# The tail of a decode block: gate's matmuls on two columns scaled afterwards, the last two heads straight into wo's rows, and the last diagonal in halves

## The chip, the cores and the metric

The kernel runs on one core of a Trainium2 chip. The metric is device time in microseconds (us); each timed run is one execution of the whole kernel, and the median of several is compared.

## The reference

One token goes through a conditioned transformer block: D = 640, 32 heads of 128, a cache of 16384 positions for each head, and a feed-forward layer of F = 1728.

```python
mod = silu(c) @ w_mod                         # six vectors: sa, ca, ga, sb, cb, gb
h = layernorm(x) * (1 + ca) + sa
q = h @ wq                                    # 32 heads x 128
o[head] = softmax(q[head] @ K[head].T / sqrt(128)) @ V[head]
x = x + ga * (concat(o) @ wo)
h = layernorm(x) * (1 + cb) + sb
x = x + gb * ((silu(h @ w_gate) * (h @ w_up)) @ w_down)
```

The caches are 268 of the 290 MB that are read.

## The kernel before

Every operation is recorded with the operations that it depends on, and each engine then runs its own in the order in which the program recorded them. An engine waits for a semaphore of another engine, or of a transfer, before an instruction that needs it. The order on each engine is therefore the order of the source, and an instruction whose input is late holds back all that stand behind it on that engine.

Heads go in 16 pairs. For a pair, K (8.4 MB) is loaded into one of two buffers (`load_k`), DVE multiplies it by q and folds it (`score`), PE finishes the sum (`reduce_mm`), and the largest score and the exponentials follow (`largest`, `weigh`). V (8.4 MB) has a single buffer, so its load waits until PE has read the V before it (`load_v`). `pv` multiplies the weights by V into `acc_ps`, ACT copies that to `acc_sb` (L473), and `diag` picks each head's own part with small float32 matmuls into `OT_ps` (L482). Pairs 1 to 14 run in a loop on PE; pair 15 (`PL`, `NP - 1`) is written out, with its V loaded in four pieces.

All large loads are issued by SP in the order of the source. In the last stretch that is: V of pair 14, `dma_wo0` (24 heads' rows) and `dma_wo3` (8 heads' rows) after the scores of pair 14, the four pieces of the last V once PE has finished with V of pair 14, and after the scores of pair 15 gate's weights (`dma_wg`), up's in two pieces (`dma_wu0`, `dma_wu1`) and down's in four (`dma_wd0` to `dma_wd3`).

The product with wo needs the heads' outputs laid out as wo's rows were loaded. `GROUPS` says how: a group (h0, n) holds n heads, and each partition holds n consecutive rows of wo, 1280 bytes each. The outputs are divided by their sums (`on`), spread by a mask into `Z` on DVE (`z_op`, L617), turned by a matmul each (`lay`, L630), copied to `A_sb` by ACT (L633), and then multiplied by wo (`project`, L645: five matmuls of one column for each head, all into `attn_ps`). The first four groups are done while the last V is on its way. Group 4, heads 28 to 31, waits for the last pair: on_last, z, am, as, and 20 matmuls.

Then ACT copies the attention output (`attn_bf`, L688), DVE scales it by `ga` and adds x, and `layernorm_ops` (L360 to L377) makes the second normalisation: PE sums over partitions (`ln2_tot`, L362), DVE centres (`ln2_xc`, L364), ACT squares (L367), PE sums again (`ln2_tot2`, L369), ACT takes Ln and Exp for the reciprocal deviation (L371, L374). DVE scales and shifts (L694, L697) to `h2_col`, clears the sums of gate and up (L698, L699), and PE multiplies by gate (70 matmuls of one column), up (56 and 14; all at L709) and, after the silu on ACT and DVE, by down (L730, four groups of 20, 20, 20 and 10, each of which waits for its own piece of the weights).

Of the kernel before, what the change touches and what calls it, by code (L numbers as in the profile page):

```python
# [6 lines left out]
BF16 = mybir.dt.bfloat16  # L7
# [200 lines left out]
def build(nc, A_x, A_k, A_v, A_wq, A_wo, B_wg, B_wu, B_wd, c_in, w_mod, out):  # L208
    H, S, Dh = A_k.shape[1], A_k.shape[2], A_k.shape[3]
    D = A_x.shape[2]  # L210
# [10 lines left out]
    assert FT % 2 == 0 and FT // 2 <= 128  # L221
    FR = FT // 2
    FCH = 4 * NB + 2
    GROUPS = [(0, 8), (8, 8), (16, 8), (24, 4), (28, 4)]
    QW = 32
    QR = 16

# [1 line left out]
    with es:  # L229
# [5 lines left out]
        def sb(name, shape, dtype):  # L235
            return es.enter_context(nc.sbuf_tensor(name, list(shape), dtype))
# [20 lines left out]
        negid = sb("negid", [128, 64], F32)  # L257
        d2 = sb("d2", [128, 64], F32)
        sel = sb("sel", [128, 8], F32)
        msk = {n: sb("msk%d" % n, [128, 128 // n], F32) for n in (8, 4)}  # L260
        e8 = {n: sb("e%d" % n, [128, n], BF16) for n in (8, 4)}
        Z = sb("Z", [128, H // 8 + 1, 128], BF16)
        A_sb = sb("A_sb", [128, H], BF16)
        rows = sb("rows", [1, 2, D], BF16)
        pm = sb("pm", [128, NP], F32)
        nb = sb("nb", [128, NP], F32)
        rsz = sb("rsz", [128, H], F32)
# [20 lines left out]
        tt2 = sb("tt2", [128, KC], F32)  # L288
        tt3 = sb("tt3", [128, KC], F32)
        h2_col = sb("h2_col", [128, KC], BF16)  # L290
        eg = sb("eg", [128, FCH], F32)
        dg = sb("dg", [128, FCH], F32)
        rg = sb("rg", [128, FCH], F32)
# [63 lines left out]
        o_rr = op(DVE, lambda e: e.reciprocal(out=rr[:], in_=dd[:]), deps=[o_dd], name="rr")  # L357
        o_sc = op(DVE, lambda e: e.tensor_tensor(out=silu_c[:], in0=c_col[:], in1=rr[:], op=ALU.mult), deps=[o_rr, o_cc], name="silu_c")

        def layernorm_ops(src_f32, src_dep, sum_ap, c0, tag, xc_t, free=None):  # L360
            st_ps = misc
            o_tot = op(PE, lambda e: e.matmul(st_ps[:, c0:c0 + 1], lhsT=ones_f[:], rhs=sum_ap, start=True, stop=True),  # L362
                       deps=[src_dep, o_onesf, free], name=tag + "_tot")
            o_xc = op(DVE, lambda e: e.scalar_tensor_tensor(  # L364
                out=xc_t[:], in0=src_f32[:], scalar=float(D), in1=st_ps[:, c0:c0 + 1].broadcast_to([128, KC]),
                op0=ALU.mult, op1=ALU.subtract), deps=[o_tot, src_dep], name=tag + "_xc")
            o_sq = op(ACT, lambda e: e.activation(  # L367
                out=junk[:], in_=xc_t[:], func=ACTF.Square, accum_out=st[:, c0 + 1:c0 + 2]), deps=[o_xc], name=tag + "_sq")
            o_tot2 = op(PE, lambda e: e.matmul(st_ps[:, c0 + 1:c0 + 2], lhsT=ones_f[:], rhs=st[:, c0 + 1:c0 + 2], start=True, stop=True),  # L369
                        deps=[o_sq], name=tag + "_tot2")  # L370
            o_ln = op(ACT, lambda e: e.activation(  # L371
                out=st[:, c0 + 2:c0 + 3], in_=st_ps[:, c0 + 1:c0 + 2], func=ACTF.Ln, scale=1.0 / float(D) ** 3, bias=EPS),
                deps=[o_tot2], name=tag + "_ln")
# [37 lines left out]
        o_h = op(DVE, lambda e: e.tensor_tensor(out=h_col[:], in0=tt1[:], in1=mod_ps[:, 0:KC], op=ALU.add), deps=[o_t1], name="h_col")  # L411
        o_modc = op(ACT, lambda e: e.activation(out=modb[:], in_=mod_ps[:, 2 * KC:6 * KC], func=ACTF.Copy), deps=[o_mod, o_h], name="mod_b")
        o_onep_b = op(DVE, lambda e: e.tensor_scalar_add(out=onep_b[:], in0=modb[:, 2 * KC:3 * KC], scalar1=1.0), deps=[o_modc], name="onep_b")
        ga, sb_, gb = modb[:, 0:KC], modb[:, KC:2 * KC], modb[:, 3 * KC:4 * KC]


# [42 lines left out]
        def pv(p):  # L459
            cuts = VCUT if p == NP - 1 else [0, T2]  # L460
            prev = None
            for c, (a, b) in enumerate(zip(cuts, cuts[1:])):
                def f_pv(e, p=p, a=a, b=b):
                    last = None
                    for j in range(a // 4, b // 4):
                        s = j % 4
                        last = e.matmul(acc_ps[32 * s:32 * s + 8, :], lhsT=PZ[:, p % 2, j, :],  # L467
                                        rhs=vbuf[:, 4 * j:4 * j + 4, :].rearrange("p t d -> p (t d)"),
                                        start=(j < 4), stop=(j >= NCH - 4), tile_position=(0, 32 * s))
                    return last  # L470
                prev = op(PE, f_pv, deps=[o_exp[p], d_v[p][c], o_acc[p - 1] if p >= 1 else o_accz, prev], name="pv%d_%d" % (p, c))
            o_pv[p] = prev
            o_acc[p] = op(ACT, lambda e: e.activation(out=acc_sb[:], in_=acc_ps[:], func=ACTF.Copy),  # L473
                          deps=[o_pv[p], o_diag[p - 1] if p >= 1 else None], name="acc%d" % p)

# [2 lines left out]
        def diag(p):  # L478
            def f_diag(e):
                last = None  # L480
                for i in range(4):
                    last = e.matmul(OT_ps[:, 0:2], lhsT=acc_sb[:, 128 * i:128 * (i + 1)], rhs=sel[:, i:8:4],  # L482
                                    start=(i == 0), stop=(i == 3))
                return last
            o_diag[p] = op(PE, f_diag, deps=[o_acc[p], o_sel, o_ot[p - 1] if p >= 1 else o_xf], name="diag%d" % p)
            if p < NP - 1:
                o_ot[p] = op(ACT, lambda e: e.activation(  # L487
                    out=OT_sb[:, 2 * p:2 * p + 2], in_=OT_ps[:, 0:2], func=ACTF.Copy), deps=[o_diag[p]], name="ot%d" % p)

        def reduce_mm(p, c, fold):  # L490
            def f_R(e):
# [87 lines left out]
        while a < len(GROUPS):  # L579
# [7 lines left out]
            for i in range(a, b):  # L587
                d_wo[i] = d
            a = b

# [57 lines left out]
            return op(PE, f_wo, deps=[o_as[g], d_wo[g]] + o_qev[-1], name="wo%d" % g)  # L648

        NG = len(GROUPS)  # L650
        lay(list(range(NG - 1)))
# [20 lines left out]

        for g in range(NG - 1):
            project(g)
        pv(NP - 1)
        diag(NP - 1)
        o_onl = op(DVE, lambda e: e.tensor_tensor(out=on_f[:, LAST:H], in0=OT_ps[:, 0:2], in1=rl[:, LAST:H], op=ALU.mult),  # L679
                   deps=[o_rl, o_diag[NP - 1]], name="on_last")  # L680
        for g, o in z_op(LAST, H, o_onl, "b"):
            o_z.setdefault(g, []).append(o)
        lay([NG - 1])
        o_wo = project(NG - 1)

        o_abf = op(ACT, lambda e: e.activation(out=attn_bf[:], in_=attn_ps[:, 0:KC], func=ACTF.Copy), deps=[o_wo], name="attn_bf")  # L688
# [4 lines left out]
        o_xc1, o_rstd1 = layernorm_ops(x1, o_x1, st[:, 4:5], 4, "ln2", xc1, o_rl)  # L693
# [4 lines left out]
        o_zg = op(DVE, lambda e: e.memset(g_ps[:, 0:FCH], 0.0), deps=[o_exp[NP - 2]], name="zero_g")  # L698
        o_zu = op(DVE, lambda e: e.memset(u_ps[:, 0:FCH], 0.0), deps=[o_exp[NP - 1]], name="zero_u")  # L699

        def chunk(j):
            return (slice(512 * (j // 4) + j % 4, 512 * (j // 4) + 512, 4), 128) if j < 4 * NB else (slice(512 * NB + j % 4, F, 2), FR)

        def f_gu(e, wv, ps_t, k0, k1):
            last = None
            for k in range(k0, k1):
                for j in range(FCH):
                    cols, w = chunk(j)
                    last = e.matmul(ps_t[0:w, j:j + 1], lhsT=wv[:, k, cols], rhs=h2_col[:, k:k + 1],  # L709
                                    start=(k == 0 and j == 0), stop=(k == KC - 1 and j == FCH - 1), skip_group_check=True)  # L710
            return last
        o_g = op(PE, lambda e: f_gu(e, wg_v, g_ps, 0, KC), deps=[o_h2, d_wg, o_zg], name="gate")
        o_u0 = op(PE, lambda e: f_gu(e, wu_v, u_ps, 0, UK), deps=[o_h2, d_wu[0], o_zu], name="up0")
        o_u = op(PE, lambda e: f_gu(e, wu_v, u_ps, UK, KC), deps=[o_h2, d_wu[1], o_u0], name="up1")
        o_eg = op(ACT, lambda e: e.activation(out=eg[:], in_=g_ps[:, 0:FCH], func=ACTF.Exp, scale=-1.0), deps=[o_g], name="eg")
        o_dg = op(DVE, lambda e: e.tensor_scalar_add(out=dg[:], in0=eg[:], scalar1=1.0), deps=[o_eg], name="dg")
        o_rg = op(DVE, lambda e: e.reciprocal(out=rg[:], in_=dg[:]), deps=[o_dg], name="rg")
        o_sg = op(DVE, lambda e: e.tensor_tensor(out=sg[:], in0=g_ps[:, 0:FCH], in1=rg[:], op=ALU.mult), deps=[o_rg, o_g], name="sg")
# [67 lines left out]
```

## Time and profile before

| | |
|---|---|
| median of 3 runs | 686.59 us (686.27 to 686.76) |
| the profiled execution, its own time | 686.55 us |
| its span in the profile | 684.6 us |
| outside the span | 1.95 us |
| granted TensorE clock, mean | 0.60 |
| DVE busy | 509.8 us, 74% |
| PE busy | 366.3 us, 54% |
| read from HBM | 290.47 MB, 424 GB/s over the span |
| packets of SP's queue | 98.4% of 16 engines' time |

The span is the time from the first to the last instruction of the profiled execution; its own time has what lies around it as well. All positions below are microseconds from the span's start. In the stretches after 640 us the granted clock is 0.50. The chain of waits is followed back from the last instruction, and each step of it is what released the one after it.

### The profile page before, as it was taken

To read this page: it belongs to the slowest core of one execution; us is meant where nothing else is said; L and a number is where in the kernel's file an instruction comes from. 1 tells how busy PE (TensorE), PEld (TensorE's weight loads), DVE (VectorE), ACT (ScalarE), POOL (GpSimd) and SP (SyncE) were. 2 spreads that over 40 slices of the span, in tenths; PEclk is the share of its full clock that TensorE was granted. 3 is DMA by queue.
4 is the path that set the end of the run, shared out by engine and by line. 5 is a ranking of instruction groups with operands and counts; after the bars stand their busy time and mean duration, and the time that the engine had idled before them with its cause. 6 is when DMAs were issued, how large, how long until landed. Compare 5 with 4: busy or idle time off the path is not lost.

```text
span 684.6 us, 5113 instructions
## 1 busy us (share of the span) xinstructions
PE 366.3 (54%) x2282; PEld 152.5 (22%) x2283; DVE 509.8 (74%) x179; ACT 45.8 (7%) x145; POOL 0.7 (0%) x6
## 2 busy tenths in 40 slices
PE   2522265646648173756637183745638184654765
PEld 2311122222212021221212121221212122222525
DVE  2079998959595977959595987959596986999200
ACT  1120000000000000100000000100000000100100
POOL 0000000000000000000000000000000000000000
PEclk9975565655556565565656565655656565655655
DMA  9999999999999999999999999999999999999994
GB/s 381 427 458 426 429 429 429 434 433 429 460 437 433 429 429 433 433 429 429 429 437 433 429 452 444 433 429 429 433 429 433 429 429 433 425 440 414 430 421 169
DMA packets 7422, 290.62 MB, mean 425 GB/s; under 512 B 914, under 2 KB 916, under 8 KB 1908
## 3 DMA queue, kind: packets, MB, share of 16 engines
q1 hardware_dynamic: 7408, 290.48, 98.4%
q8 instruction: 7, 0.11, 0.1%
q14 instruction: 3, 0.02, 0.0%
q10 hardware_dynamic: 4, 0.00, 0.0%
HBM read 290.47 MB, written 0.00 MB: 424 GB/s over the span
## 4 chain that ended last, share of the span: by engine, by line
DMA 52%; DVE 35%; PE 12%; issue 0%; ACT 0%; SPq 0%; DVEq 0%
DMA kring<-in_A_k_cache_dram 44%; DVE kring L503 16%; DVE kring L507 8%; DMA vbuf<-in_A_v_cache_dram 8%; PE psb L494 7%; DVE kring L512 4%; DVE kring L518 3%; DVE kring L524 2%; PE psb L467 2%; PE psb L709 1%; PE psb L532 1%; PE psb L730 0%; DVE pm L538 0%; PE psb L482 0%; SPq L80 0%
## 5 line engine op out<-in xcount | busy, mean ns | idle before, releaser
L503 DVE TENSOR_TENSOR kring<-kring,qbc 128x16384 bf16<-128x16384 bf16 x28 | 243.3, 8689 | 95.0 <-DMA kring<-in_A_k_cache_dram 95.0
L494 PE MATMUL psb<-kring,ident 128*128 128x256 bf16 x448 | 197.4, 607 | 124.1 <-DVE kring L512 124.1
L507 DVE TENSOR_TENSOR kring<-kring 128x8192 bf16<-128x8192 bf16 x28 | 123.8, 4420 | 0.5
L494 PEld LDWEIGHTS psb<-kring,ident 128*128 128x128 bf16 x448 | 51.7, 121 | 254.0 <-DVE kring L512 133.7
L467 PE MATMUL psb<-vbuf,PZ 128*8 128x512 bf16 x1024 | 84.6, 500 | 11.7 <-DMA vbuf<-in_A_v_cache_dram 11.5
L542 PE MATMUL psb<-d,bd_f 128*128 128x64 f32 x32 | 11.0, 447 | 113.8 <-ACT d L540 113.8
L512 DVE TENSOR_TENSOR kring<-kring 128x4096 bf16<-128x4096 bf16 x28 | 64.0, 2287 | 0.5
L518 DVE TENSOR_TENSOR kring<-kring,qbc 128x16384 bf16<-128x16384 bf16 x4 | 34.7, 8687 | 16.2 <-DMA kring<-in_A_k_cache_dram 16.2
L467 PEld LDWEIGHTS psb<-vbuf,PZ 128*8 128x8 bf16 x1024 | 27.3, 105 | 73.2 <-issue 53.4
L542 PEld LDWEIGHTS psb<-d,bd_f 128*128 128x128 f32 x32 | 8.0, 311 | 115.5 <-DVE pm L538 58.1
L532 PE MATMUL psb<-kring,ident 128*128 128x128 bf16 x64 | 14.5, 393 | 35.9 <-DVE kring L524 35.9
L524 DVE TENSOR_TENSOR kring<-kring 128x8192 bf16<-128x8192 bf16 (+2 forms) x12 | 31.7, 2646 | 0.3
L482 PEld LDWEIGHTS psb<-sel,acc_sb 128*128 128x128 f32 x128 | 29.3, 319 | 8.4 <-issue 4.3
L482 PE MATMUL psb<-sel,acc_sb 128*128 128x2 f32 x128 | 26.4, 328 | 1.4 <-ACT acc_sb L473 1.4
L473 ACT ACTIVATE acc_sb<-psb 128x512 f32<-128x512 f32 x16 | 9.6, 597 | 222.2 <-PE psb L467 222.2
L550 ACT ACTIVATE PZ<-psb,nb 64x256 bf16<-64x256 f32 x32 | 15.0, 469 | 63.0 <-DVE nb L546 62.8
L532 PEld LDWEIGHTS psb<-kring,ident 128*128 128x128 bf16 x64 | 7.4, 121 | 42.3 <-DVE kring L524 37.0
L679 DVE TENSOR_TENSOR on_f<-psb,rl 128x2 f32<-128x2 f32 x1 | 0.2, 159 | 20.6 <-PE psb L482 20.6
L540 ACT ACTIVATE d<-negid,pm 128x64 f32<-128x64 f32 x16 | 5.6, 348 | 139.1 <-DVE pm L538 139.1
L426 PE MATMUL psb<-vbuf,h_col 128*128 128x512 bf16 x39 | 10.1, 425 | 7.8 <-DMA vbuf<-in_A_wq_dram 7.8
L487 ACT ACTIVATE OT_sb<-psb 128x2 f32<-128x2 f32 x15 | 2.6, 172 | 158.5 <-PE psb L482 158.5
L403 PE MATMUL psb<-silu_c,kring 128*128 128x1 bf16 x150 | 6.2, 178 | 4.5 <-DMA kring<-in_w_mod_dram 4.5
(82 smaller groups left out, 86.2 us busy)
## 6 DMA issues: line engine op xcount, KB each, us to landing
kring<-in_A_k_cache_dram SPq DMA_DIRECT2D x4, 4096.0 KB, 37.6
vbuf<-in_A_wq_dram SPq DMA_DIRECT2D x1, 5120.0 KB, 27.1
kring<-in_w_mod_dram SPq DMA_DIRECT2D x1, 4800.0 KB, 14.1
vbuf<-in_A_v_cache_dram SPq DMA_DIRECT2D x1, 4096.0 KB, 16.4
kring<-in_A_wo_dram SPq DMA_DIRECT2D x1, 3840.0 KB, 29.2
kring<-in_B_w_gate_dram SPq DMA_DIRECT2D x1, 2160.0 KB, 25.9
vbuf<-in_A_v_cache_dram SPq DMA_DIRECT2D x1, 2048.0 KB, 20.9
kring<-in_B_w_down_dram SPq DMA_DIRECT2D x3, 640.0 KB, 32.6
```

What stands on the lines that cost most here:

```text
L426: last = e.matmul(q_ps[b][:, 0:512], lhsT=h_col[:, k:k + 1].broadcast_to([128, 128]), rhs=wq_v[:, k, g * 512:(g + 1) * 512], start=(k == 0 ...
L467: last = e.matmul(acc_ps[32 * s:32 * s + 8, :], lhsT=PZ[:, p % 2, j, :], rhs=vbuf[:, 4 * j:4 * j + 4, :].rearrange("p t d -> p (t d)"), st ...
L482: last = e.matmul(OT_ps[:, 0:2], lhsT=acc_sb[:, 128 * i:128 * (i + 1)], rhs=sel[:, i:8:4], start=(i == 0), stop=(i == 3))
L494: last = e.matmul(S_ps[p % 2][:, 0:T2], lhsT=ident[:], rhs=kring[:, p % 2, :, d], start=(d == 0), stop=(d == QW + QR - 1))
L503: o_m = op(DVE, lambda e: e.tensor_tensor(out=kv4, in0=kv4, in1=q4, op=ALU.mult), deps=[d_k[p][-1]] + o_qev[p // 2], name="mult%d_%d" % (p ...
L507: o_f = op(DVE, lambda e: e.tensor_tensor(out=kv4[:, :, 0], in0=kv4[:, :, 0], in1=kv4[:, :, 1], op=ALU.add), deps=[o_m], name="fold%d_%d" ...
L512: return op(DVE, lambda e: e.tensor_tensor(out=lo[:, :, 0:QR], in0=lo[:, :, 0:QR], in1=lo[:, :, QR:QW], op=ALU.add), deps=[o_f], name="fol ...
L518: o = op(DVE, lambda e: e.tensor_tensor(out=kv, in0=kv, in1=qbc[:, p, :].unsqueeze(1).broadcast_to([128, KCUT[c + 1] - KCUT[c], 128]), op= ...
L524: o = op(DVE, lambda e, w=w: e.tensor_tensor(out=kv[:, :, 0:w], in0=kv[:, :, 0:w], in1=kv[:, :, w:2 * w], op=ALU.add), deps=[o], name="fol ...
L532: last = e.matmul(S_ps[p % 2][:, KCUT[c]:KCUT[c + 1]], lhsT=ident[:], rhs=kring[:, p % 2, KCUT[c]:KCUT[c + 1], d], start=(d == 0), stop=(d ...
L542: o_mx[p] = op(PE, lambda e: e.matmul(mx_ps[:, 0:64], lhsT=bd_f[:], rhs=d2[:], start=True, stop=True), deps=[o_d2, o_bd1, o_bd2, o_nb[p - ...
L550: o_exp[p] = op(ACT, lambda e, half=half, ps=ps: e.activation(out=PZ[ps, p % 2, :, 4 * half:4 * half + 4], in_=S_ps[p % 2][ps, 0:T2].rearr ...
```

## The change

Five things change, and all but the first are in the last stretch.

- At the start, the two input rows are kept in the space of `qbc`, a third mask and selector (for n = 2) are made on DVE, and the shift of the second normalisation is copied to the second column of a new tile `ab` (640 x 2 values as 128 x 5 x 2).
- The last group of `GROUPS` shrinks to heads 28 and 29, so wo's last 1280 KB come in three transfers: 640 KB (group 3, 5120 bytes a partition), 320 KB (group 4, 2560 bytes a partition) and the last two heads as 320 KB, one row of 1280 bytes for each partition and head (`dma_wol`). All 30 heads are laid out and multiplied before the last V's products.
- The last pair's copy of `acc_ps` and its diagonal are done in two halves. on_last writes the divided outputs straight into `A_sb`, and ten matmuls (`wo_last`) finish the product.
- attn_bf is made by DVE instead of ACT, and the two clearing memsets stand before it.
- Gate is no longer multiplied by the finished `h2_col`, but by two columns side by side: the centred input times (1 + cb), and the shift. The first 14 of its matmuls (`gate0`) stand on PE between ln2's two totals, the other 56 after the second. Two operations on DVE then scale the first result by the reciprocal deviation and add the second. Up still uses `h2_col`.

```diff
-    GROUPS = [(0, 8), (8, 8), (16, 8), (24, 4), (28, 4)]
+    GROUPS = [(0, 8), (8, 8), (16, 8), (24, 4), (28, 2)]
...
+        o_abs = op(DVE, lambda e: e.tensor_copy(out=ab[:, :, 1], in_=modb[:, KC:2 * KC]), deps=[o_modc], name="ab_shift")
...
             o_sq = op(ACT, lambda e: e.activation(
                 out=junk[:], in_=xc_t[:], func=ACTF.Square, accum_out=st[:, c0 + 1:c0 + 2]), deps=[o_xc], name=tag + "_sq")
+            if between:
+                between(o_xc)
             o_tot2 = op(PE, ...)
...
+        def diag_last():
+            p, last = NP - 1, o_diag[NP - 2]
+            copies = [op(ACT, lambda e, h=h: e.activation(
+                out=acc_sb[:, 256 * h:256 * h + 256], in_=acc_ps[:, 256 * h:256 * h + 256], func=ACTF.Copy),
+                deps=[o_pv[p], last], name="acc%d_%d" % (p, h)) for h in range(2)]
+            for h in range(2):
+                def f_diag(e, h=h):
+                    out = None
+                    for i in (2 * h, 2 * h + 1):
+                        out = e.matmul(OT_ps[:, 0:2], lhsT=acc_sb[:, 128 * i:128 * (i + 1)], rhs=sel[:, i:8:4],
+                                       start=(i == 0), stop=(i == 3))
+                    return out
+                o_diag[p] = op(PE, f_diag, deps=[copies[h], o_sel, o_ot[p - 1]], name="diag%d_%d" % (p, h))
+            return o_diag[p]
...
+        d_wol = dma(wo_v[:, H - 2:H, :], A_wo[(H - 2) * 128:H * 128, :].rearrange("(h p) n -> p h n", p=128), "wol", deps=[o_R[NP - 2]], name="dma_wol")
...
-        pv(NP - 1)
-        diag(NP - 1)
-        o_onl = op(DVE, lambda e: e.tensor_tensor(out=on_f[:, LAST:H], in0=OT_ps[:, 0:2], in1=rl[:, LAST:H], op=ALU.mult),
-                   deps=[o_rl, o_diag[NP - 1]], name="on_last")
-        for g, o in z_op(LAST, H, o_onl, "b"):
-            o_z.setdefault(g, []).append(o)
-        lay([NG - 1])
-        o_wo = project(NG - 1)
+        pv(PL)
+        o_onl = op(DVE, lambda e: e.tensor_tensor(out=A_sb[:, LAST:H], in0=OT_ps[:, 0:2], in1=rl[:, LAST:H], op=ALU.mult),
+                   deps=[o_rl, diag_last()], name="on_last")
+        def f_wol(e):
+            last = None
+            for k in range(LAST, H):
+                for cc in range(KC):
+                    last = e.matmul(attn_ps[:, cc:cc + 1], lhsT=wo_v[:, k, cc:D:KC], rhs=A_sb[:, k:k + 1],
+                                    start=False, stop=(k == H - 1 and cc == KC - 1), skip_group_check=True)
+            return last
+        o_wo = op(PE, f_wol, deps=[o_onl, d_wol], name="wo_last")
...
-        o_abf = op(ACT, lambda e: e.activation(out=attn_bf[:], in_=attn_ps[:, 0:KC], func=ACTF.Copy), deps=[o_wo], name="attn_bf")
+        o_zg = op(DVE, lambda e: e.memset(g_ps[:, 0:2 * FCH], 0.0), deps=[o_exp[NP - 2]], name="zero_g")
+        o_zu = op(DVE, lambda e: e.memset(u_ps[:, 0:FCH], 0.0), deps=[o_exp[NP - 1]], name="zero_u")
+        o_abf = op(DVE, lambda e: e.tensor_copy(out=attn_bf[:], in_=attn_ps[:, 0:KC]), deps=[o_wo], name="attn_bf")
...
+        def gate0(o_xc1):
+            o_a = op(DVE, lambda e: e.tensor_tensor(out=ab[:, :, 0], in0=xc1[:], in1=onep_b[:], op=ALU.mult),
+                     deps=[o_xc1, o_onep_b, o_abs], name="ab_a")
+            o_g0.append(op(PE, lambda e: f_gu(e, wg_v, g_ps, ab_f, 2, 0, 1), deps=[o_a, d_wg, o_zg], name="gate0"))
+        o_xc1, o_rstd1 = layernorm_ops(x1, o_x1, st[:, 4:5], 4, "ln2", xc1, o_rl, gate0)
...
-        o_g = op(PE, lambda e: f_gu(e, wg_v, g_ps, 0, KC), deps=[o_h2, d_wg, o_zg], name="gate")
+        o_g = op(PE, lambda e: f_gu(e, wg_v, g_ps, ab_f, 2, 1, KC), deps=o_g0, name="gate")
...
+        gp = g_ps[:, 0:2 * FCH].rearrange("p (j n) -> p j n", n=2)
+        o_gt = op(DVE, lambda e: e.tensor_scalar_mul(out=sg[:], in0=gp[:, :, 0], scalar1=st[:, 7:8]), deps=[o_g, o_rstd1], name="gate_r")
+        o_gs = op(DVE, lambda e: e.tensor_tensor(out=g_sb[:], in0=gp[:, :, 1], in1=sg[:], op=ALU.add), deps=[o_gt], name="gate_s")
+        o_eg = op(ACT, lambda e: e.activation(out=eg[:], in_=g_sb[:], func=ACTF.Exp, scale=-1.0), deps=[o_gs], name="eg")
```

More of the change, by code (lines that the diff above doesn't have):

```diff
@@ L259, in build @@
         sel = sb("sel", [128, 8], F32)
-        msk = {n: sb("msk%d" % n, [128, 128 // n], F32) for n in (8, 4)}
-        e8 = {n: sb("e%d" % n, [128, n], BF16) for n in (8, 4)}
+        msk = {n: sb("msk%d" % n, [128, 128 // n], F32) for n in (8, 4, 2)}
+        e8 = {n: sb("e%d" % n, [128, n], BF16) for n in (8, 4, 2)}
         Z = sb("Z", [128, H // 8 + 1, 128], BF16)
         A_sb = sb("A_sb", [128, H], BF16)
-        rows = sb("rows", [1, 2, D], BF16)
+        rows = qbc[0:1].rearrange("p a d -> p (a d)")[:, 0:2 * D].rearrange("p (j n) -> p j n", j=2)
         pm = sb("pm", [128, NP], F32)
@@ L290, in build @@
         h2_col = sb("h2_col", [128, KC], BF16)
+        ab = sb("ab", [128, KC, 2], BF16)
+        g_sb = sb("g_sb", [128, FCH], F32)
         eg = sb("eg", [128, FCH], F32)
@@ L358, in build, with layernorm_ops @@
         o_sc = op(DVE, lambda e: e.tensor_tensor(out=silu_c[:], in0=c_col[:], in1=rr[:], op=ALU.mult), deps=[o_rr, o_cc], name="silu_c")
-        def layernorm_ops(src_f32, src_dep, sum_ap, c0, tag, xc_t, free=None):
+        def layernorm_ops(src_f32, src_dep, sum_ap, c0, tag, xc_t, free=None, between=None):
             st_ps = misc
@@ L472, in pv @@
             o_pv[p] = prev
+            if p == NP - 1:
+                return
             o_acc[p] = op(ACT, lambda e: e.activation(out=acc_sb[:], in_=acc_ps[:], func=ACTF.Copy),
@@ L485, in diag @@
             o_diag[p] = op(PE, f_diag, deps=[o_acc[p], o_sel, o_ot[p - 1] if p >= 1 else o_xf], name="diag%d" % p)
-            if p < NP - 1:
-                o_ot[p] = op(ACT, lambda e: e.activation(
-                    out=OT_sb[:, 2 * p:2 * p + 2], in_=OT_ps[:, 0:2], func=ACTF.Copy), deps=[o_diag[p]], name="ot%d" % p)
+            o_ot[p] = op(ACT, lambda e: e.activation(
+                out=OT_sb[:, 2 * p:2 * p + 2], in_=OT_ps[:, 0:2], func=ACTF.Copy), deps=[o_diag[p]], name="ot%d" % p)
+        def diag_last():
[12 more added lines that the diff above has]
+            return o_diag[p]
         def reduce_mm(p, c, fold):
@@ L650, in build @@
         NG = len(GROUPS)
-        lay(list(range(NG - 1)))
+        lay(list(range(NG)))
         largest(PL)
@@ L671, in build @@
                         B_wd[512 * NB:F, :].rearrange("(p r) n -> p (r n)", r=2), ("wd", NB), deps=wdeps, name="dma_wd%d" % NB))
-        for g in range(NG - 1):
+        for g in range(NG):
             project(g)
-        pv(NP - 1)
-        diag(NP - 1)
-        o_onl = op(DVE, lambda e: e.tensor_tensor(out=on_f[:, LAST:H], in0=OT_ps[:, 0:2], in1=rl[:, LAST:H], op=ALU.mult),
-                   deps=[o_rl, o_diag[NP - 1]], name="on_last")
-        for g, o in z_op(LAST, H, o_onl, "b"):
-            o_z.setdefault(g, []).append(o)
-        lay([NG - 1])
-        o_wo = project(NG - 1)
-        o_abf = op(ACT, lambda e: e.activation(out=attn_bf[:], in_=attn_ps[:, 0:KC], func=ACTF.Copy), deps=[o_wo], name="attn_bf")
+        pv(PL)
[12 more added lines that the diff above has]
+        o_abf = op(DVE, lambda e: e.tensor_copy(out=attn_bf[:], in_=attn_ps[:, 0:KC]), deps=[o_wo], name="attn_bf")
         o_ga = op(DVE, lambda e: e.tensor_tensor(out=tt2[:], in0=attn_bf[:], in1=ga, op=ALU.mult), deps=[o_abf, o_modc], name="ga_attn")
@@ L692, in build, with chunk, f_gu @@
             deps=[o_ga, o_xf], name="x1")
-        o_xc1, o_rstd1 = layernorm_ops(x1, o_x1, st[:, 4:5], 4, "ln2", xc1, o_rl)
+        def chunk(j):
+            return (slice(512 * (j // 4) + j % 4, 512 * (j // 4) + 512, 4), 128) if j < 4 * NB else (slice(512 * NB + j % 4, F, 2), FR)
+        def f_gu(e, wv, ps_t, src, n, k0, k1):
+            last = None
+            for k in range(k0, k1):
+                for j in range(FCH):
+                    cols, w = chunk(j)
+                    last = e.matmul(ps_t[0:w, n * j:n * j + n], lhsT=wv[:, k, cols], rhs=src[:, n * k:n * k + n],
+                                    start=(k == 0 and j == 0), stop=(k == KC - 1 and j == FCH - 1), skip_group_check=True)
+            return last
+        ab_f = ab[:].rearrange("p k n -> p (k n)")
+        o_g0 = []
+        def gate0(o_xc1):
[3 more added lines that the diff above has]
+        o_xc1, o_rstd1 = layernorm_ops(x1, o_x1, st[:, 4:5], 4, "ln2", xc1, o_rl, gate0)
         o_t2 = op(DVE, lambda e: e.scalar_tensor_tensor(
@@ L697, in build @@
         o_h2 = op(DVE, lambda e: e.tensor_tensor(out=h2_col[:], in0=tt3[:], in1=sb_, op=ALU.add), deps=[o_t2], name="h2_col")
[L698 to L711, printed above, removed]
@@ L712, in build @@
-        o_g = op(PE, lambda e: f_gu(e, wg_v, g_ps, 0, KC), deps=[o_h2, d_wg, o_zg], name="gate")
-        o_u0 = op(PE, lambda e: f_gu(e, wu_v, u_ps, 0, UK), deps=[o_h2, d_wu[0], o_zu], name="up0")
-        o_u = op(PE, lambda e: f_gu(e, wu_v, u_ps, UK, KC), deps=[o_h2, d_wu[1], o_u0], name="up1")
-        o_eg = op(ACT, lambda e: e.activation(out=eg[:], in_=g_ps[:, 0:FCH], func=ACTF.Exp, scale=-1.0), deps=[o_g], name="eg")
+        o_g = op(PE, lambda e: f_gu(e, wg_v, g_ps, ab_f, 2, 1, KC), deps=o_g0, name="gate")
@@ new lines, in build @@
+        o_u0 = op(PE, lambda e: f_gu(e, wu_v, u_ps, h2_col, 1, 0, UK), deps=[o_h2, d_wu[0], o_zu], name="up0")
+        o_u = op(PE, lambda e: f_gu(e, wu_v, u_ps, h2_col, 1, UK, KC), deps=[o_h2, d_wu[1], o_u0], name="up1")
+        gp = g_ps[:, 0:2 * FCH].rearrange("p (j n) -> p j n", n=2)
+        o_gt = op(DVE, lambda e: e.tensor_scalar_mul(out=sg[:], in0=gp[:, :, 0], scalar1=st[:, 7:8]), deps=[o_g, o_rstd1], name="gate_r")
+        o_gs = op(DVE, lambda e: e.tensor_tensor(out=g_sb[:], in0=gp[:, :, 1], in1=sg[:], op=ALU.add), deps=[o_gt], name="gate_s")
@@ L716, in build @@
+        o_eg = op(ACT, lambda e: e.activation(out=eg[:], in_=g_sb[:], func=ACTF.Exp, scale=-1.0), deps=[o_gs], name="eg")
         o_dg = op(DVE, lambda e: e.tensor_scalar_add(out=dg[:], in0=eg[:], scalar1=1.0), deps=[o_eg], name="dg")
         o_rg = op(DVE, lambda e: e.reciprocal(out=rg[:], in_=dg[:]), deps=[o_dg], name="rg")
-        o_sg = op(DVE, lambda e: e.tensor_tensor(out=sg[:], in0=g_ps[:, 0:FCH], in1=rg[:], op=ALU.mult), deps=[o_rg, o_g], name="sg")
+        o_sg = op(DVE, lambda e: e.tensor_tensor(out=sg[:], in0=g_sb[:], in1=rg[:], op=ALU.mult), deps=[o_rg, o_gs], name="sg")
```

## The prediction

> **What bounds the kernel now.** I read the 40 slices first: the transfers are busy throughout, so until the last V arrives nothing but the transfers counts.
>
> ```profile
> DMA  9999999999999999999999999999999999999994
> GB/s 381 427 458 426 429 429 429 434 433 429 460 437 433 429 429 433 433 429 429 429 437 433 429 452 444 433 429 429 433 429 433 429 429 433 425 440 414 430 421 169
> ```
>
> Next the chain that ended last, from 600 us on. The columns are start, length and what ran.
>
> ```profile
> 635.13 24.13 DMA vbuf<-in_A_v_cache_dram
> ...
> 661.56 0.61 ACT acc_sb L473
> ...
> 662.21 1.88 PE psb L482 x8
> ...
> 664.38 0.24 DVE Z L617
> ...
> 664.66 0.20 PE psb L630
> ...
> 664.88 0.18 ACT A_sb L633
> ...
> 665.11 0.97 PE psb L645 x20
> 666.08 0.02 issue
> 666.11 0.19 ACT attn_bf L688
> ...
> 669.62 5.17 PE psb L709 x126
> 674.80 0.14 issue
> 674.93 0.70 PE psb L709 x14
> ...
> 678.15 0.95 PE psb L730 x20
> ```
>
> The V of the last pair lands at 659.26 (635.13 + 24.13), and from there every step waits for the one before it: 25 us of tail. Third, the issues of the weights, to see which later landing stands close to its use (KB, us from issue to landing).
>
> ```profile
> kring<-in_B_w_gate_dram SPq DMA_DIRECT2D x1, 2160.0 KB, 25.9
> kring<-in_B_w_up_dram SPq DMA_DIRECT2D x1, 1728.0 KB, 29.6
> kring<-in_B_w_down_dram SPq DMA_DIRECT2D x1, 640.0 KB, 33.9
> kring<-in_B_w_down_dram SPq DMA_DIRECT2D x1, 240.0 KB, 28.1
> ```
>
> The timeline of SP has gate issued at 639.74 and the first up at 640.11, so they land at 665.64 and 669.7. The issues of wd begin at 641.06; the stretches place the third at 642.0 (its issue takes 6.2 us, and the fourth begins at 648.3), so the four land at 672.4, 674.1, 675.9 and 676.4. The matmuls that use them (L730) began at 675.96, 677.07, 678.15 and 679.23. The third has 2.25 us to spare, the least of the four. Transfers are thus a second path that runs beside the tail.
>
> **The sum, step by step,** in times of the profiled run, first with all landings left where they are.
>
> Diagonal in halves. The 0.61 us copy of 512 columns becomes two of 256. The 64x256 eviction at L433 took 378 ns, two back to back 0.78 us. So the first half is there at 661.56 + 0.38 = 661.94, the diagonal starts 0.04 later at 661.98 (was 662.21), and the second copy (done at 662.34) is hidden under the first half's matmuls (half of 1.88 us). End 663.86, gain 0.23. If a break of 0.14 us came between the halves, as between the groups of L730, 0.09 would be left. I take 0.23: those groups wait for their predecessor on PE, the second half waits only for ACT.
>
> Last heads straight into wo's rows. on_last keeps its 0.17 us and writes A_sb, ending at 664.12. Away go Z (0.24), am (0.20), as (0.18) and their hops: from on_last's end (664.35) to wo's start (665.11) was 0.76 us and becomes one hop of 0.04. wo's 20 matmuls (0.97) become 10; ten of L730 took 0.55. So wo_last runs 664.16 to 664.71. attn_bf moves from ACT (0.19) to DVE (a five-column PSUM read there took 165 ns, L734) and costs the same within 0.03. ga_attn starts at 664.92 instead of 666.32: 1.40 us gained so far.
>
> What these two heads' neighbours pay is off the path. Group 28 to 29 now joins the early lay-out: one Z of 286 instead of 222 ns, one more am of 0.05, ten more matmuls before the V arrives (0.042 each, from 140 in 5.85 us: 0.42). PE had been done at 648.9 and waits for V until 650.7, so 0.5 of 1.8 us cover is used. The two added issues of wo pieces (0.45 us each) stand on SP at 609 to 610.5 after the wait for R14 that wo already has; SP's next instruction, the last V, is at 634.27. Two more reductions at the start (0.28 each) and one five-column copy (0.17) fall into DVE's idle stretches 12.4 to 21.1 and 22 to 38. Without that cover they would cost their 0.7 us.
>
> Gate early. From ga_attn to the end of xc nothing changes, so xc ends at 667.54 - 1.40 = 666.14. Then ab_a (hop 0.02, a five-column product 0.17, hop 0.04) lets gate0 start at 666.37; wg landed at 665.64, 0.7 us ahead. 14 matmuls at 41 ns (126 in 5.17 us) take 0.58. A second moving column is not in the trace: rows of 128 and 256 columns (L532: 16 in 3.63 us, L494: 16 in 7.05) differ by 1.7 ns a column, the 1, 4 and 8 column matmuls by nothing. I take 1.7 ns, 0.02 here and 0.12 over all 70. gate0 ends at 666.97. ln2_tot2 is queued behind it on PE: its input is ready at 666.5, so it is held back some 0.5 us, and ln, rstd, t2 and h2 behind it. tot2 takes 0.60, to 667.57; those four (0.95 us with hops) are done at 668.5. Nobody waits for that: PE meanwhile has the 56 matmuls left of gate (2.30 + 0.10) until 669.97, and only up0 wants h2. up0 also wants wu0 (669.7), which is just there. up0 takes 2.30, up1 0.14 + 0.70: end 673.11 (was 675.64). gate_r, gate_s, eg, dg, rg, sg (1.3 us by their rows) lie under up's 3.1 us. The two memsets that stood ahead of gate (0.12) now lie under wo_last; without that cover they are 0.1 us. With gu as before (0.32) down0 starts at 673.43, a gain of 2.53 us, of which gate's part is 1.13.
>
> Then the other path. down0 and down1 (at 674.54) find their rows landed, at 672.4 and 674.1. down2 would start at 675.62, but its rows land at 675.9: it starts at 675.95. The fourth's are there when down3 comes. So 678.15 - 675.95 = **2.20 us** is left of 2.53: a stall of 0.33 moves to down2's wait for its transfer, and that is late next.
>
> The transfers themselves. wo's last 1280 KB went in 256 packets of 5120 B; now 128 of 5120, 128 of 2560 and 256 of 1280: 256 more, 16 for each of 16 engines, ahead of the last V in the queue. They cannot bring anything earlier, the bytes being the same. Their price comes from these stretches:
>
> ```profile
> DMA packets 162, 1.67 MB, mean 416 GB/s; under 512 B 0, under 2 KB 0, under 8 KB 0
> DMA packets 79, 2.59 MB, mean 431 GB/s; under 512 B 0, under 2 KB 0, under 8 KB 0
> DMA packets 97, 0.30 MB, mean 295 GB/s; under 512 B 18, under 2 KB 18, under 8 KB 96
> ```
>
> At 630 to 634 us a packet of 10.3 KB took 4 x 16 / 162 = 395 ns; at the 431 GB/s of the large ones (642 to 648) its bytes need 382, so 13 ns go on the packet. The 5 KB packets of 636 to 638 give 12. That is 16 x 13 = **0.2 us**, on every landing from the last V to wd and so on the whole end. Upper bound: the slowest stretch (673 to 674, 168 ns a packet where the bytes need 113) gives 55 ns, 0.9 us. I take 0.2, the wo packets themselves. The Trainium skill (DMA: Bandwidth & Descriptors, Why small descriptors are slow) puts the overhead at about three cycles a packet; with the 850 MHz of its bandwidth section that would be an estimated 0.06 us here, less than the rows give, and the sum 0.15 better.
>
> Net: 2.20 - 0.20 = 2.0 us. The profiled execution took 686.55 (span 684.6 and 1.95 around it), the median is 686.59; so 684.6.
>
> **Rivals.**
> The landings give way: with wd2 0.33 earlier, or the packets free, the whole 2.53 counts: 684.1 to 684.3. For it: the wait is small beside the scatter of landings; the transfers run at under half share after 674, so the last landing hangs on few engines. Against: 33.9 us is what was measured. 14%.
>
> Gate gives nothing: two columns cost PE more than a third extra, or wg slips past 666.4 and gate0 holds ln2_tot2 and with it everything. It decides from 1.1 us on. What is left is 1.40 - 0.20: 685.4. Against: the 1 to 8 column rows are alike, wg has 0.7 us to spare. 14%.
>
> Slower: the last V comes late behind the cut-up wo. The only tiny transfer in the trace, the output with 128 packets of its own, took 4.0 us from issue to landing. If the two added pieces cost 2 us each in the queue instead of being overlapped, all landings move by 4.0: 686.59 - 2.20 + 4.0 = 688.4. It decides from 2.2 us on, 0.14 us per added packet of an engine. Against: the 512 KB piece of the last V landed 1.25 us after the piece ahead of it (635.56 + 24.9 against 659.26), which is its bytes at 420 GB/s and no fixed cost. 9%. The Trainium skill (the same page, Anatomy of one DMA, and Bandwidth) gives about 2.0 us fixed per transfer for GpSimd's path and tells one to batch to 1 MiB; taken serially that would be the same estimated 4.0 us, but the row just quoted speaks against it for this queue.
>
> **The numbers.** The forecast itself has 63%. What a measurement of this kernel can tell is 0.2%, 1.37 us, so 685.22 and 687.96 are the bounds. Faster: forecast, the first rival and a remainder of the second, 80%. Same: the rest of the second and packets near 0.9 us, 11%. Slower 9%. The range reaches from 683.8 (whole 2.53, no packet cost, 0.25 scatter of the runs shown) to 685.7 (gate worthless, packets dear).
>
> **What would show it.** The chain after: acc_sb copy near 0.38 us, no Z, am or as after the diagonal, ten wo matmuls, ga_attn about 1.4 us nearer to the last V; gate0 between ln2's two totals; down2 or down3 idle for in_B_w_down. The 1280-byte packets show as packets under 2 KB, up from 916 by 256, and as the last V landing about 659.5. I am wrong if V lands past 661.5, if PE waits for wg, or if the 70 gate matmuls take over 3.5 us.

## The result and the profile after

The changed kernel takes 684.35 us (684.17 to 684.79, 7 runs) beside 686.59 for the kernel before: 2.24 us less, ratio 0.9969 [0.9958, 0.9981]. Its profiled execution took 684.17 with a span of 682.5. Times differ by up to 0.7 us from chip to chip (the kernel before had 686.0 to 686.7), so each experiment below is given as the difference to the kernel before on its own chip.

The page of the profile after, transfers and packets:

```profile
DMA  9999999999999999999999999999999999999995
GB/s 384 423 461 427 430 430 431 427 430 431 434 434 434 446 446 438 430 434 430 430 434 430 430 430 434 430 430 430 430 434 434 438 446 442 413 455 392 430 418 222
DMA packets 7711, 290.63 MB, mean 426 GB/s; under 512 B 946, under 2 KB 1204, under 8 KB 2196
```

Packets between 512 B and 2 KB went from 2 to 258 (1204 - 946), the 256 of the last two heads. The 32 more under 512 B come with the two more transfers; the one more load of `e10_busy` below brought 16 (930 where the kernel before has 914). Now the chain that ended last, its last part (start, length):

```profile
643.07 33.49 DMA kring<-in_B_w_down_dram
676.56 0.05 issue
676.61 0.97 PE psb L767 x20
677.58 0.14 issue
677.71 0.55 PE psb L767 x10
```

Before, this chain ran from the landing of the last V through every step of the tail. Now it jumps from the third of down's transfers (issued at 643.07, landed at 676.56) to the matmuls that use it. The tail's own steps, from the timeline after:

```profile
661.82 0.66 ACT L499 ACTIVATE acc_sb<-psb 128x256 f32<-128x256 f32 x2 [18.03 <-PE psb L472]
662.25 1.87 PE L506 MATMUL psb<-sel,acc_sb 128*128 128x2 f32 x8 [0.48 <-ACT acc_sb L499]
664.23 0.16 DVE L701 TENSOR_TENSOR A_sb<-psb,rl 128x2 bf16<-128x2 f32 x1 [19.59 <-PE psb L506]
664.44 0.56 PE L708 MATMUL psb<-A_sb,kring 128*128 128x1 bf16 x10 [0.32 <-DVE A_sb L701]
665.05 0.17 DVE L717 CAST attn_bf<-psb 128x5 bf16<-128x5 f32 x1 [0.56 <-PE psb L708]
...
666.72 0.72 PE L731 MATMUL psb<-ab,kring 128*128 128x2 bf16 x14 [0.46 <-DVE ab L738]
667.30 0.56 PE L373 MATMUL psb<-st,ones_f 128*128 128x1 f32 x2
667.73 2.36 PE L731 MATMUL psb<-ab,kring 128*128 128x2 bf16 x56
670.17 3.19 PE L731 MATMUL psb<-h_col,kring 128*128 128x1 bf16 x70
673.70 0.96 PE L767 MATMUL psb<-gu_col,kring 128*128 128x1 bf16 x20 [0.34 <-DVE gu_col L756]
675.09 0.96 PE L767 MATMUL psb<-gu_col,kring 128*128 128x1 bf16 x20 [0.44 <-DMA kring<-in_B_w_down_dram]
676.61 1.64 PE L767 MATMUL psb<-gu_col,kring 128*128 128x1 bf16 x30 [0.55 <-DMA kring<-in_B_w_down_dram]
```

One sees the two half copies, no Z, am or as between the diagonal and wo's ten matmuls, gate0 (14 x two columns) ahead of ln2's second total (L373), and two waits of down for its own rows, ahead of the second and the third group. In a second profile of the changed kernel (`a2_after`) only the third group waited, because the second's rows had landed at 674.68:

```profile
673.81 0.96 PE L767 MATMUL psb<-gu_col,kring 128*128 128x1 bf16 x20 [0.34 <-DVE gu_col L756]
674.92 0.93 PE L767 MATMUL psb<-gu_col,kring 128*128 128x1 bf16 x20
676.56 0.96 PE L767 MATMUL psb<-gu_col,kring 128*128 128x1 bf16 x20 [0.71 <-DMA kring<-in_B_w_down_dram]
```

### The profile page after: what moved, and what is told of

Read it like the earlier page. It is cut to its first block, busy times and chain, and to the rows that moved or that the text cites. A ratio compares the mean times of both kernels' runs of the same rounds, so it can differ in the third digit from the quotient of the medians.

```text
span 682.5 us, 5119 instructions
## 1 busy us (share of the span) xinstructions
PE 373.7 (55%) x2282; PEld 154.4 (23%) x2283; DVE 510.8 (75%) x185; ACT 45.5 (7%) x144; POOL 0.7 (0%) x6
## 2 busy tenths in 40 slices
DMA packets 7711, 290.63 MB, mean 426 GB/s; under 512 B 946, under 2 KB 1204, under 8 KB 2196
## 4 chain that ended last, share of the span: by engine, by line
DMA 54%; DVE 35%; PE 10%; SPq 0%; issue 0%; ACT 0%
DMA kring<-in_A_k_cache_dram 44%; DVE kring L525 16%; DVE kring L529 8%; PE psb L516 7%; DMA kring<-in_B_w_down_dram 5%; DMA vbuf<-in_A_v_cache_dram 4%; DVE kring L534 4%; DVE kring L540 3%; DVE kring L546 2%; PE psb L472 2%; PE psb L554 1%; SPq L80 0%; DVE pm L560 0%; PE psb L767 0%; PE psb L489 0%
## 5 line engine op out<-in xcount | busy, mean ns | idle before, releaser
L472 PE MATMUL psb<-vbuf,PZ 128*8 128x512 bf16 x1024 | 91.2, 531 | 11.3 <-DMA vbuf<-in_A_v_cache_dram 11.1
L472 PEld LDWEIGHTS psb<-vbuf,PZ 128*8 128x8 bf16 x1024 | 29.0, 110 | 77.8 <-issue 62.8
L489 PEld LDWEIGHTS psb<-sel,acc_sb 128*128 128x128 f32 x120 | 27.5, 318 | 7.2 <-issue 4.3
L489 PE MATMUL psb<-sel,acc_sb 128*128 128x2 f32 x120 | 24.5, 326 | 0.7 <-ACT acc_sb L480 0.7
```

## The experiments

**The two parts apart.** `e1_heads` has gate as before:

```diff
-        o_xc1, o_rstd1 = layernorm_ops(x1, o_x1, st[:, 4:5], 4, "ln2", xc1, o_rl, gate0)
+        o_xc1, o_rstd1 = layernorm_ops(x1, o_x1, st[:, 4:5], 4, "ln2", xc1, o_rl)
...
-        o_g = op(PE, lambda e: f_gu(e, wg_v, g_ps, ab_f, 2, 1, KC), deps=o_g0, name="gate")
+        o_g = op(PE, lambda e: f_gu(e, wg_v, g_ps, h2_col, 1, 0, KC), deps=[o_h2, d_wg, o_zg], name="gate")
...
```

> The change without its gate part: gate is multiplied by the finished h2_col again, one column, behind ln2's second total. Theory (the end is the later of two paths, the chain behind the last V and the landings of down's rows): the chain gains 1.40 us, the added packets cost 0.25, the landings of down's rows are not reached, so 1.15 below the kernel before: 685.4; no down group waits for its transfer. Rival (the heads part carries nearly all, gate's part is worth little): 684.6 or less. Rival (the cut-up wo costs much and gate pays for it): 686 or more.

Measured: 684.95 beside 686.03, 1.08 less (1.15 had been expected), ratio 0.9982 [0.9973, 0.9991]; no group of down waited for its rows. `e2_gate` is the kernel before with gate0, the two columns and the scaling afterwards, and with wo, the last heads and the diagonal untouched.

> The gate part alone, put into the kernel before: two columns, gate0 between the two totals, scaled afterwards; wo's transfers, the last heads and the diagonal as before. Theory: the chain gains 1.13 us, nothing else moves: 685.45, last V where it was, no wait for down's rows (about 1.1 us to spare). Rival (gate's part is worth little): 686.3. Rival (landings already bind): under 0.7 us gained and a wait for in_B_w_down in the profile.

Measured: 684.68, 1.35 less (1.13 had been expected), ratio 0.9979 [0.9970, 0.9988]; no wait for down's rows. Neither part is worthless; alone they add up to 2.43, a little more than both together.

**Is it one chain or two?** `e3_whole` takes the halves of the diagonal back, 0.2 us of chain:

```diff
-            copies = [op(ACT, ... out=acc_sb[:, 256 * h:256 * h + 256] ...) for h in range(2)]
+            o_c = op(ACT, lambda e: e.activation(out=acc_sb[:], in_=acc_ps[:], func=ACTF.Copy), deps=[o_pv[p], last], name="acc%d" % p)
...
```

> The change with the last diagonal whole again: one copy of 512 columns, one diagonal. The chain is 0.2 us longer. Theory (in the changed kernel the last groups of down wait for their rows, so 0.2 on the chain is covered): the same as the changed kernel within 0.1, 684.35, and down's wait for its rows shorter by 0.2. Rival (one chain sets the end): 0.2 later, 684.55.

Measured: 683.91 beside 686.03, 2.12 less, where the changed kernel had 2.24 and, when run again, 2.03. So the halves are worth nothing that can be told here; down's third group began at 676.26, straight after its rows had landed. `e5_wol_late` goes the other way and shortens the chain:

```diff
-        d_wol = dma(wo_v[:, H - 2:H, :], ...)      # ahead of the last V
...
         load_v(PL)
+        d_wol = dma(wo_v[:, H - 2:H, :], ...)
```

> The changed kernel with the transfer of the last two heads' wo rows issued behind the last V, and nothing else. The last V lands 0.7 us earlier, and the chain up to gu is 0.7 earlier. Theory (down's last landings set the end): the same as the changed kernel within 0.15, with a longer wait ahead of down's second and third group. Rival (the chain behind the last V sets the end): 0.7 below the changed kernel.

Measured: 684.52 beside 686.68, 2.16 less, the same as the changed kernel although the last V's third piece landed at 658.55 instead of 659.5 to 659.6. The timeline of PE shows where that 1 us went:

```profile
665.96 0.70 PE L731 MATMUL psb<-ab,kring 128*128 128x2 bf16 x14 [0.66 <-DMA kring<-in_B_w_gate_dram]
...
670.08 3.19 PE L731 MATMUL psb<-h_col,kring 128*128 128x1 bf16 x70 [0.80 <-DMA kring<-in_B_w_up_dram]
673.61 0.96 PE L767 MATMUL psb<-gu_col,kring 128*128 128x1 bf16 x20 [0.34 <-DVE gu_col L756]
674.84 0.96 PE L767 MATMUL psb<-gu_col,kring 128*128 128x1 bf16 x20 [0.27 <-DMA kring<-in_B_w_down_dram]
676.44 1.64 PE L767 MATMUL psb<-gu_col,kring 128*128 128x1 bf16 x30 [0.64 <-DMA kring<-in_B_w_down_dram]
```

Each weight in turn is now waited for: gate, up, and down twice. A faster chain only buys waits.

**What the waits for down's rows cost.** `e4_nowd` and its control `e8_nowd_before` let down read rows that are long there:

```diff
-                        last = e.matmul(f_ps[:, cc:cc + 1], lhsT=wd_v[0:w, j, cc:D:KC], ...
+                        last = e.matmul(f_ps[:, cc:cc + 1], lhsT=wg_v[0:w, j % KC, cc:D:KC], ...
-            prev = op(PE, f_down, deps=[o_gum, d_wd[b], prev, o_nb[NP - 1]], name="down%d" % b)
+            prev = op(PE, f_down, deps=[o_gum, d_wg, prev, o_nb[NP - 1]], name="down%d" % b)
...
```

> The changed kernel in which down multiplies rows of gate's weights (landed long before) instead of its own; down's own rows are still loaded, and only the end of the kernel waits for them. So nothing waits for down's rows on PE; the values are other ones. Theory: down2 starts 0.7 us earlier than in the changed kernel, 683.65; the last row of down lands before the end. Rival (the waits for down's rows cost nothing in most executions): 684.35.

> The kernel before in which down multiplies rows of gate's weights (landed long before) instead of its own; down's own rows are still loaded, only the end of the kernel waits for them; the values are other ones. Control for the same edit on the changed kernel, which took 0.9 us off. Theory (in the kernel before, down's rows are there 2 us before they are wanted): no change, within 0.15 of the kernel before. Rival (that edit saves something else, such as waiting instructions or reads of other rows): 0.5 to 0.9 faster here as well.

Measured: on the changed kernel 682.89 beside 686.03, 3.14 less and so 1.0 below `e3_whole` on the same chip. The control, expected to do nothing, was 0.30 faster (685.74 beside 686.04, ratio 0.9996 [0.9987, 1.0005], which leaves no change inside). Its chain of waits shows part of it:

```profile
675.88 0.97 PE psb L730 x20
676.85 0.05 issue
676.89 0.97 PE psb L730 x20
677.86 0.05 issue
677.91 0.97 PE psb L730 x20
```

In the kernel before, 0.14 us of issue stands between these groups (as at 674.80 in the lines of the prediction), though the rows had landed 2 to 3 us earlier. Each group there waits for two semaphores, PE's own and the transfer's; with the transfer's taken away the break is 0.05, and the group reads 0.02 longer. From the start of down's first group to the end of its last it is 3.81 us in the kernel before and 3.62 in both kernels without these waits: 0.19 of the 0.30. The same stretch is 4.43 in `e3_whole`, so of the 1.0 us of `e4_nowd` 0.62 are the waits for the rows (0.7 had been expected) and 0.19 the shorter breaks; the rest is about what the output's transfer gave, 3.23 us instead of 3.48.

**What small packets cost.** `e6_rows` loads wo's first eight heads row by row:

```diff
+            if a == 0:
+                for k in range(8):
+                    d = dma(wo_v[:, k:k + 1, :], A_wo[0:8 * 128, :].rearrange("(p k) n -> p k n", k=8)[:, k:k + 1, :], ...
```

> The changed kernel with wo's first group (8 heads, 1280 KB) loaded in single rows of 1280 bytes by eight transfers, instead of 10240 bytes a packet: 896 more packets, 56 for each of 16 engines. By the traces so far (the stretch from the first wo landing to the last V grew by 0.15 us for 16 packets an engine, 9 ns each) the last V and down's rows land 0.5 us later, and so does the end: 684.35 + 0.5 on the scale of the first measurement, 0.5 above the changed kernel. By the 13 ns of the forecast 0.7. Rival (small packets or separate transfers are dear, 55 ns a packet or 2 us a transfer): 3 us or more. Rival by the three cycles a packet that the Trainium skill gives (DMA: Bandwidth & Descriptors, Why small descriptors are slow): an estimated 0.2.

Measured: 683.91 beside 686.04, 2.13 less, so no cost at the end that can be told from the changed kernel's scatter: the 0.5 was expected there and missed. The landings do show it. The last V's third piece came at 659.69, where two kernels with uncut wo on the same chip had 659.14 and 659.16: 0.54 us for 72 added packets an engine (16 of the change and these 56), 7 to 8 ns each. Down's third piece landed 0.54 to 0.58 later than in those two as well (676.80 beside 676.22 and 676.26); the end does not show it, but there the output took only 2.80 us to land. The dear-packet rival is out by a factor of seven.

**A better version.** `e9_split` adds to `e5_wol_late` a cut of down's third transfer:

```diff
+        DCUT = [0, 4, 8, 10, 12, FCH]
+        for b in range(4):
+            r0, r1 = DCUT[b], DCUT[b + 1]
+            blk = B_wd[512 * (r0 // 4):512 * (r0 // 4) + 512, :].rearrange("(p r) n -> p r n", r=4)
+            d_wd.append(dma(wd_v[:, r0:r1, :], blk[:, r0 % 4:r0 % 4 + r1 - r0, :], ("wd", b), deps=wdeps, name="dma_wd%d" % b))
...
```

> The changed kernel with the transfer of the last two heads' wo rows issued behind the last V, and the third transfer of down's rows cut into two of two rows each, with down in five groups of 20, 20, 10, 10 and 10 matmuls. Theory (the end is down's last landings plus the matmuls that are left then): the last V lands 0.7 us earlier, which gains nothing by itself; the matmuls left after the third piece's landing fall from 1.6 us to about 1.1, so 0.3 to 0.5 below the changed kernel. Rival (the chain behind the last V sets the end): 0.7 below. Rival (smaller packets at the end make the landings late): no gain.

Measured: 682.75 (682.58 to 682.80) beside 686.04: 3.29 less, ratio 0.9951 [0.9938, 0.9965], about 1.1 below the changed kernel and the best of all. End of its chain:

```profile
652.16 24.18 DMA kring<-in_B_w_down_dram
...
676.42 0.55 PE psb L769 x10
...
677.11 0.55 PE psb L769 x10
```

Behind the landing at 676.34 stand 20 matmuls instead of 30, and the output is issued at 678.07 instead of 678.67. That is 0.6 of the 1.1, a little more than the 0.3 to 0.5 expected; the rest lies behind the issue of the output, whose transfer took 2.62 us here, the shortest of all, and what sets that is not known. The cut without the reordering was not run.

**The output's transfer.** In the span of the profiled execution the output's landing gave 0.6 us that the prediction did not have. The issue views of before and after:

```profile
out_dram<-o_col SPq DMA_DIRECT2D x1, 1.2 KB, 4.0
```

```profile
out_dram<-o_col SPq DMA_DIRECT2D x1, 1.2 KB, 3.4
```

Four runs went after this. `e10_busy` puts one more load between down's rows and the output:

```diff
+        d_more = dma(vbuf[:, 0:32, :], v_src(0)[:, 0:32, :], "more", deps=[o_pv[NP - 1]], name="dma_more")
...
```

> The kernel before with one more load of 1 MB (a piece of V that nobody uses), issued by SP behind all others once the last V has been read; only the end of the kernel waits for it. It ends about 2.4 us after down's last row, some 1.3 us ahead of the output's issue. In the profiles so far the output took 4.0 us to land where the transfers had been idle for 3.8 us before it, 3.8 at 1.9 to 2.2, 3.4 to 3.5 at 1.6, 3.2 at 0.9. Theory (a transfer lands sooner when the queue has been busy shortly before): the output lands in 3.3 to 3.5 us and the kernel is 0.4 to 0.6 faster than before although it loads more. Rival (the idle time has nothing to do with it): 4.0 and no change, or later if the load hinders the output.

Measured: 685.73 beside 686.04, ratio 0.9995 [0.9986, 1.0004]: not told from no change, where 0.4 to 0.6 had been expected. The load landed at 679.49, 0.6 us ahead of the output's issue, and the output took 3.2 us. Then both kernels once more, for second profiles:

> The changed kernel once more, beside the kernel before on the same chip, for a second profile. Theory (two errors of the forecast cancelled: down's third piece landed 0.5 later than forecast, and the output's transfer was 0.6 shorter than in the profile of before): 2.1 to 2.3 below the kernel before; the output again lands in 2.6 to 3.5 us; down2 again waits and starts 1.4 to 1.8 earlier than in the kernel before. Rival (the short output transfer was an accident of that one profile): it lands in 3.6 to 4.0 and down2 starts 2.0 earlier.

> The kernel before once more, for a second profile of it. Theory (the output takes longer where the transfers have been idle for over 2 us): it lands in 3.4 to 4.0 us. Rival (the output's time is scatter, the same in all kernels): anywhere from 2.6 to 4.0; below 3.2 would speak for it. The time is that of the kernel before.

Measured: the changed kernel 684.65, 2.03 below 686.68 (2.1 to 2.3 had been expected; ratio 0.9970 [0.9958, 0.9982]), the kernel before 686.74 (1.0001 [0.9992, 1.0010]). The output took 4.06 us after and 4.53 before, both outside what was expected. down's third group began at 676.56 after and at 678.25 before, 1.7 earlier, having waited. Last, `e12_delay` holds the changed kernel's output back:

```diff
+        def f_more(e):
+            last = None
+            for i in range(40):
+                last = e.matmul(A_ps[:, 64 + i:65 + i], lhsT=wg_v[:, 0, i % 5:640:5], rhs=gu_col[:, 0:1], start=True, stop=True)
+            return last
+        prev = op(PE, f_more, deps=[prev], name="more")
```

> The changed kernel with 40 more matmuls of one column behind down, into a bank that nobody reads; the last two operations of DVE wait for them. That holds the output's issue back by about 2.1 us, to 680.7, 0.5 later than in the kernel before (680.2 to 680.3), and leaves the transfers idle for 3.8 us ahead of it, as there. On each of four chips the output landed 0.4 to 0.6 us sooner in kernels whose end waits for down's rows than in kernels whose end does not. Theory (it is the idle time ahead of the output that makes it longer): the output takes as long as in the kernel before, and the time is 0.4 to 0.6 above the kernel before. Rival (the shorter output belongs to the changed kernel, whatever the idle time): 0.5 shorter, and the time equals the kernel before within 0.15.

Measured: 685.62 beside 686.10, ratio 0.9993 [0.9984, 1.0002]. The matmuls took 1.76 us, so the output was issued at 680.05 and not at 680.7, and landed in 3.26. The issue was thus 0.15 to 0.25 earlier than in the two profiles of the kernel before (680.19, 680.29). The idle theory then wanted 0.15 to 0.25 less than the kernel before and its rival 0.65 to 0.75; the measured 0.48 lies between. The output's time runs from 2.6 to 4.5 us over the 14 profiles and differs by chip. Among kernels on one chip it was on average 0.4 to 0.7 shorter where the output followed down's landings within 1.8 us than where it came later without an added load, on all four chips that had both; but the added load of `e10_busy` shortened it only by 0.2 against `e8_nowd_before`. What sets it stays open.

## Why the prediction was right

The forecast was 684.6 for 684.35 measured, faster, within the range. One reading first: what the prediction calls the landing of the last V is that of its third piece. The fourth landed at 660.48, 1.23 us later and not 1.25, but ahead of its use at 660.91, so the chain stands. By its steps:

**Last heads and diagonal.** From the end of pv to ga_attn took 4.78 us before (661.54 to 666.32) and takes 3.45 after (661.80 to 665.25): 1.33 gained, 1.40 forecast. The diagonal's 0.23 came out at 0.21 in the profile, and as nothing in the time, since the end waits for the landings.

**Gate.** From the end of xc to down0 took 8.42 before (667.54 to 675.96), 7.23 after (666.47 to 673.70): 1.19, forecast 1.13. Sizes were off against each other. Alone (`e2_gate`) the stretch is 7.00, so 1.42; in its chain of waits stand

```profile
667.60 0.71 PE psb L708 x14
668.32 0.43 PE psb L373 x2
668.74 4.45 PE psb L708 x112
```

These are 5.59 us where the forecast had counted 5.90. ln2_tot2 loads its weights while gate0 still runs and adds 0.43, not 0.60, and no price of the second column shows (in the second profile of the changed kernel 56 matmuls of two columns took 2.34 us, up's 56 of one column 2.36), where 0.12 had been set aside. In the changed kernel wu0 (up's first piece), "just there" in the forecast, is there too late by a hair: it landed at 670.03 when gate's last matmul was running, and gate and up no longer run through as one (112 matmuls in 4.45 us in `e2_gate`).

**Packets.** From the landing of the first wo transfer to that of the last V's third piece:

| kernels | us |
|---|---|
| wo as before (before, again, `e2_gate`, `e8_nowd_before`, `e10_busy`) | 21.46, 21.47, 21.46, 21.48, 21.46 |
| wo cut up (after, again, `e1_heads`, `e3_whole`, `e4_nowd`, `e12_delay`) | 21.60, 21.62, 21.63, 21.63, 21.60, 21.59 |

0.15 us, where 0.20 was forecast from the 10 KB packets: 9 ns for each of 16 packets, with whatever the two added transfers cost themselves included. The rule of the Trainium skill (DMA: Bandwidth & Descriptors, Why small descriptors are slow) had given an estimated 0.06; the runs lie between the two, nearer to the rows. The rival of dear packets or transfers is refuted here and by `e6_rows`. The Trainium skill's advice in the same page (Bandwidth) to batch to 1 MiB is not borne out on this queue, where transfers stand one behind another: pieces of 320 KB landed 0.84 and 0.89 us apart (639.49, 640.33, 641.22), which is their bytes at 390 and 368 GB/s where the large packets had 431.

**The other path.** The forecast had down2 (down's third group) wait 0.33 for its rows and start at 675.95 + 0.20 = 676.15. It did wait, but until 676.56 (676.51 in the second profile), and in the first profile down1 had waited too, until 675.05. This term was mis-sized. From the last V's third piece to this landing the profile of before shows 16.66 us, and it was the shortest of all: the others with wo as before have 16.86 to 17.12, the changed kernel 17.05 and 16.87. A single profile's landing was taken as fixed. The rival in which the landings give way was wrong in its direction: they bind more, and 2.53 us of chain became 1.54 at down2 (678.15 to 676.61).

**The sum.** What brought the total back is not in the working: the output's 0.6 in the span, and 0.3 outside it (1.95 before, 1.67 after). 1.5 + 0.6 + 0.3 is the 2.4 between the two profiled executions. The second pair of profiles repeats it (1.66 at the output's issue, 0.47 in its transfer), but why the output lands sooner is not shown. So the sign, the parts and the bound were right by the mechanism. That 684.6 came so close to 684.35 is in part luck, errors that cancel: 0.5 us too much counted at down2, 0.9 not counted behind it.

## What to carry to other kernels

Where transfers run until shortly before the end, a tail is two paths; list every weight's landing beside its first use, and stop counting a saving where the smallest of these margins is used up. Take landings from several profiles, not one: the distance from the last V's third piece to down's third moved by 0.46 us among kernels with the same wo, more than the wait of 0.33 that was forecast. Past that point what pays is to leave little work behind the last landing: cutting one transfer of 640 KB in two, with the reordering that alone gave nothing, brought 0.6 us at the output's issue and 1.1 in the time, though the part behind the issue is not explained.

## What the hardware showed beyond that

A group of down's matmuls that waits for PE's own semaphore and for a transfer long landed starts 0.14 us after the one ahead of it; with the wait for PE's own alone it is 0.05. Over down's four groups that is 0.19 us.

SP can be held in the issue of a transfer. Before, the third and the fourth of down's transfers took 6.2 and 4.2 us to issue; after, the third took 0.43 and the fourth 11.95. The transfers stayed busy meanwhile, and nothing was seen to wait for it; what sets it is not shown.

And gate and up kept PE busy from 667 to 673, with breaks of 0.14 us at most, and the granted clock stayed at 0.50, as in the kernel before. It did not stay so everywhere after 640: in nine of the 14 profiles, the first of the changed kernel among them, it was 1.0 for 3.4 us between 652.9 and 658.5, while V's second piece was multiplied (16 matmuls of 512 columns in 1.04 us instead of 1.88). Nothing came of that, as PE waited for V's third piece either way.
